# New places for 1111 steps of an attention and mixture-of-experts kernel

## The chip, the cores and the metric

The kernel runs on one core of a Trainium2 chip. The metric is the device time of one launch in microseconds (us). The engines are TensorE (PE, with its weight load PEld), VectorE (DVE), ScalarE (ACT), GpSimd (POOL) and SyncE (SP), which here issues the loads and stores.

## What is computed

For each of 8 batches a memory attention with 8 heads, 576 tokens, head size 64 and 32 memory slots, and then a mixture of 8 experts whose choice sticks from token to token:

```python
a = softmax(phi, axis=tokens)                       # phi: [8, 8, 576, 32]
k_m = einsum('bhsm,bhsd->bhmd', a, k)
v_m = einsum('bhsm,bhsd->bhmd', a, v)
attn = softmax(q @ k_m.T / sqrt(64))                # over the 32 slots
x = (attn @ v_m), heads side by side                # [8, 576, 512]

logits = x @ w_gate                                 # 8 experts
local_gate = sigmoid(x @ w_local)
for s in range(576):
    fresh = argmax(logits[b, s])
    e = fresh if s == 0 or local_gate[b, s] < 0.5 else prev_e
    prev_e = e
    p = softmax(logits[b, s])
    out[b, s] = p[e] * (relu(x[b, s] @ w1[e]) @ w2[e])   # w1: 512x1024, w2: 1024x512
```

## The kernel before

The output of the attention is never formed. The kernel keeps the weights `at` of the attention (128 rows of heads and slots, by 576 tokens) and multiplies w1 of an expert with the keys of memory into G, so that the hidden layer is G times `at`. Both are split into a high and a low half (`Gh`, `Gl`, `ah`, `al`) and each product is made of three. Every batch computes the expert of its first token for all its tokens; a loop behind the program covers batches that need more experts.

The MoE part of a batch is a chain of matmuls on TensorE in rounds. `hidden` makes 12: four with 256 tokens and twelve matmuls each, eight with 320 tokens and six each; ScalarE and VectorE write each result as `h`. `turned` makes 32 (four output parts `dc` by eight chunks, three matmuls of 448 columns each), and behind every eighth VectorE transposes the output into `oT`. `natural` makes 8 more for the first 128 tokens. That is 52 rounds per batch and 68 for the last.

All other work stands as named steps in a table, the string `SCHEDULE`. Its first line is the prologue, run before any round; then one line is run behind each round, most of them empty. A step begins with the number of its batch. The table alone sets the order of the instructions on each engine, since nothing reorders them later; an engine takes its instructions in that order, and each waits for its operands and for the buffer it writes.

The steps that matter here, with the lines in the program: `phi`, `k`, `v` load a batch's inputs (L614), `q 0` and `q 1` sixteen pieces of q (L640), `q0 c` and `q0 d` the last parts of batch 0's q (L675, L669), all on SP's queue. `cm 0` to `cm 2` are a tree of maxima of phi on VectorE (L719), `pm`, `mc`, `pm2`, `cx` carry it across partitions (L736 to L758), `sub` and `dsub` subtract it (L763, on GpSimd and on VectorE), `pkv` sums keys and values on TensorE (L794), `pT` and `kvT` turn them, `pgg` multiplies the gate's weights with them (L866). `qT` transposes q on VectorE (L893), `psc` makes the scores (L925), `turn` transposes them (L938), and `mx`, `sub`, `exp`, `sum`, `inv`, `mul`, `at` are their softmax (L955 to L986). `a`, `z`, `o` and `p` ahead of such a name mean the part of the tokens: `a` the first nine blocks of 32, `z` the last nine; in batch 0 `o` the first block and `p` the next eight. `pl0` and `choice` take the expert of the first token (L1010, L1023 to L1025), `expert` reads it on SP (L1424), `w1` and `w2` load its weights (L1185, L1196), `pg` makes G (L1220) and `G` splits it (L1233, L1235). In batch 0 `pg` comes in four parts: `pg lo`, `pg hi`, `pg 1 lo`, `pg 1 hi`. `split` splits w2 on ScalarE and GpSimd (L1207, L1208). `warm` steps multiply zeros (L694); their results are not used.

Of the kernel before, what the change touches and what calls it, by code (L numbers as in the profile page):

```python
# [82 lines left out]


0 at store, 2 exp 1, 0 g cols, 0 gate 1, 1 a mul, 2 asum, 1 a at


1 ggt, 1 pl0, 2 q 0, 1 a ah, 1 a al, 2 q 1, 1 z psc, 1 choice, 2 pkv 0, 2 pkv 1, 2 sums, 0 gate 0, 1 z turn, 1 expert, 2 rinv, 1 w1 0, 1 w1 1
# [4 lines left out]
1 z mx  # L93
2 z qT 0, 1 z sub
2 z qT 1, 2 kvn, 2 pT, 1 pg 0, 1 w2 0, 0 gate 3, 1 z exp, 2 kvT, 0 gate 2, 1 z sum, 1 z inv, 1 z mul, 1 z at, 1 g pl, 1 g lt, 3 phi, 0 evict, 1 G 0, 2 a qT 0, 2 z psc, 1 pg 1, 1 G 1, 2 z turn, 1 split 0, 1 split 1
2 z mx
1 z ah, 1 z al, 1 split 2
# [8 lines left out]
1 g L  # L110
# [24 lines left out]
3 cx


3 sub 0, 3 exp 0, 3 a qT 0, 2 a ah  # L140
# [3 lines left out]
3 kvn, 1 gate 3

2 split 1, 2 w2 1, 2 split 2  # L150

3 pT, 3 kvT

3 a psc, 3 a turn, 3 z psc, 3 a mx, 2 at store, 3 pgg, 2 split 3, 2 split 4, 3 ggt, 4 phi, 4 colmax
1 g present, 2 split 5, 2 split 6
1 store

3 z turn
3 a sub
2 split 7, 4 q 0, 4 z qT 0
4 q 1
4 pm, 1 row store, 4 mc


3 z mx, 2 g fresh
3 a exp, 3 a sum, 3 a inv, 3 a mul, 3 a at  # L170
# [6 lines left out]
3 z sub, 2 g kept, 3 z exp  # L177
# [4 lines left out]
3 pl0, 2 g carry, 3 choice, 4 pm2  # L182
# [5 lines left out]


4 cx, 3 z sum, 4 sub 0, 3 z inv, 2 g exp, 4 kv, 2 g prob, 2 g cols  # L190

3 a ah, 3 a al

3 z mul, 3 expert, 3 w1 0, 3 w1 1, 3 z at

4 a qT 0

2 kv store, 4 exp 0, 4 sub 1, 4 exp 1, 2 gate 3
2 evict, 2 gate 1, 4 asum, 4 a qT 1, 3 pg 0, 3 G 0, 3 at store, 3 pg 1, 2 gate 2, 3 G 1, 4 pkv 0, 4 pkv 1, 3 w2 0, 4 sums, 3 w2 1, 4 z qT 1, 3 z ah, 2 gate 0
3 split 0, 3 z al, 4 rinv, 5 phi, 3 split 1, 3 split 2  # L200


4 kvn

4 pT, 4 kvT, 3 split 3
3 g pl, 3 split 4, 3 split 5, 3 split 6, 3 split 7, 4 z psc, 2 row store, 4 pgg, 4 ggt, 4 a psc, 4 z turn, 4 z mx, 4 a turn


4 a mx, 4 a sub, 4 a exp
4 a sum
# [11 lines left out]
5 kv, 4 a ah, 4 pl0, 4 choice, 3 g kept, 4 z sub  # L230
# [222 lines left out]

7 evict
# [1202 lines left out]
```

## Time and profile before

| | us |
|---|---|
| median of 3 runs | 391.22 (390.28 to 391.35) |
| profiled execution | 392.12 |
| its span in the profile | 390.3 |
| TensorE busy | 382.3 |
| VectorE busy | 285.2 |
| ScalarE busy | 170.6 |
| GpSimd busy | 157.3 |

The span runs from the first to the last instruction in the trace, and 1.8 us of the profiled execution lie around it. A busy time is the sum over an engine's instructions. An engine with a low share still decides where another engine waits for it; this is read from the waits, the stretch and the timeline, whose rows stand further below.

### The profile page before, as it was taken

The page shows a single profiled execution, that of the slowest core. Times are in us where ns is not written, and L with a number is a line of the kernel's source. Part 1 is how long each engine was busy: PE and PEld are TensorE (multiplying, and loading weights), DVE is VectorE, ACT ScalarE, POOL GpSimd, SP SyncE. Part 2 cuts the span into 40 slices and gives each one's busy share as a digit, 9 for nine tenths or more (in the row PEclk, how much of TensorE's full clock was granted, in tenths as well). Part 3 has the DMA queues.
Part 4 walks back from the last instruction along what each step waited for, and adds up shares of the span by engine and source line. Part 5 has one row for each costly group of instructions (what it writes and reads, how often), then busy time and mean ns, then how long its engine had stood idle before and what let it go on. Part 6 is the DMA issues. An engine that isn't in the chain of part 4 may idle for free. (4 is left out here: it accounts for less than half of the span.)

```text
span 390.3 us, 10303 instructions
## 1 busy us (share of the span) xinstructions
PE 382.3 (98%) x4088; PEld 329.8 (84%) x4088; DVE 285.2 (73%) x700; ACT 170.6 (44%) x430; POOL 157.3 (40%) x166
## 2 busy tenths in 40 slices
PE   8889999999999999999999999999999999999996
PEld 3658989789987998798987998879997998879995
DVE  4488769877968598666787788697896668765651
ACT  2337804276136641466205752357413753148111
POOL 1015940455026461457104673066304861336320
PEclk9989999999999999999999999999999999999999
DMA  7989798899729974997856389488797340584012
GB/s 232 265 285 395 139 265 176 268 351 325 142 101 329 268 171 179 349 304 141 273 215 225 114 165 314 135 322 226 127 359 294 123 109 16 183 267 179 0 36 91
DMA packets 119947, 82.55 MB, mean 211 GB/s; under 512 B 69972, under 2 KB 95320, under 8 KB 119896
## 3 DMA queue, kind: packets, MB, share of 16 engines
q1 hardware_dynamic: 119896, 81.86, 70.0%
q8 instruction: 33, 0.54, 0.6%
q14 instruction: 18, 0.15, 0.1%
HBM read 66.60 MB, written 15.24 MB: 210 GB/s over the span
## 5 line engine op out<-in xcount | busy, mean ns | idle before, releaser
L1208 POOL TENSOR_TENSOR w2l<-raw,w2h 128x512 fp32r<-128x512 f32 x64 | 81.4, 1298 | 49.0 <-ACT w2h L1207 28.4
L1283 PE MATMUL po<-h,w2l 128*128 128x448 f32 (+1 forms) x256 | 93.3, 365 | 0.0
L1285 PE MATMUL po<-h,w2h 128*128 128x448 f32 (+1 forms) x256 | 91.8, 359 | 0.0
L1284 PE MATMUL po<-h,w2h 128*128 128x448 f32 (+1 forms) x256 | 91.8, 359 | 0.0
L1260 DVE SCALAR_TENSOR_TENSOR h<-ph,h 128x320 fp32r<-128x320 f32 (+1 forms) x96 | 52.0, 553 | 32.5 <-ACT h L1259 32.0
L1251 PE MATMUL ph<-ah,Gh 128*128 128x256 f32 (+1 forms) x256 | 73.8, 303 | 0.0
L1251 PE MATMUL ph<-ah,Gl 128*128 128x256 f32 (+1 forms) x256 | 72.2, 296 | 0.0
L1294 POOL TENSOR_TENSOR oT<-oT,gT 128x448 f32<-128x448 f32 (+1 forms) x32 | 29.1, 925 | 85.0 <-ACT gT L1160 40.7
L1259 ACT ACTIVATE h<-ph 128x320 fp32r<-128x320 f32 (+1 forms) x96 | 46.3, 489 | 29.5 <-PE ph L1251 29.3
L1251 PE MATMUL ph<-al,Gh 128*128 128x256 f32 (+1 forms) x256 | 54.9, 295 | 0.0
L1251 PEld LDWEIGHTS ph<-ah,Gh 128*128 128x128 f32 x256 | 48.2, 188 | 4.3 <-issue 1.2
L1283 PEld LDWEIGHTS po<-h,w2l 128*128 128x128 f32 x256 | 48.3, 189 | 4.1 <-issue 0.7
L1285 PEld LDWEIGHTS po<-h,w2h 128*128 128x128 f32 x256 | 48.1, 188 | 3.6
L1284 PEld LDWEIGHTS po<-h,w2h 128*128 128x128 f32 x256 | 48.1, 188 | 3.2
L1251 PEld LDWEIGHTS ph<-ah,Gl 128*128 128x128 f32 x256 | 48.3, 189 | 0.4 <-DVE Gl L1235 0.2
L994 POOL TENSOR_TENSOR al<-at,ah 128x576 fp32r<-128x576 f32 (+1 forms) x18 | 23.7, 1319 | 44.4 <-ACT ah L990 44.2
L1251 PEld LDWEIGHTS ph<-al,Gh 128*128 128x128 f32 x256 | 41.1, 188 | 0.0
L1207 ACT ACTIVATE w2h<-raw 128x512 fp32r<-128x512 f32 x64 | 37.1, 626 | 0.1
L763 POOL TENSOR_TENSOR phi_t<-phi_t,cx 128x384 f32<-128x384 f32 (+1 forms) x13 | 18.5, 1436 | 41.5 <-ACT cx L758 30.0
L965 ACT ACTIVATE sc<-sc 128x576 f32<-128x576 f32 (+2 forms) x18 | 11.3, 631 | 47.6 <-DVE sc L960 47.6
L1268 PE MATMUL po<-w2h,h 128*128 128x512 f32 (+1 forms) x80 | 29.7, 371 | 0.0
L1269 PE MATMUL po<-w2l,h 128*128 128x512 f32 (+1 forms) x80 | 29.5, 369 | 0.0
(157 smaller groups left out, 555.9 us busy)
## 6 DMA issues: line engine op xcount, KB each, us to landing
raw<-in_moe_w_dram SPq DMA_DIRECT2D x34, 512.0 KB, 6.5
raw<-in_moe_w_dram SPq DMA_DIRECT2D x15, 1024.0 KB, 6.9
kv_t<-in_v_dram SPq DMA_DIRECT2D x7, 1152.0 KB, 9.3
kv_t<-in_k_dram SPq DMA_DIRECT2D x7, 1152.0 KB, 6.1
q_t<-in_q_dram SPq DMA_DIRECT2D x112, 72.0 KB, 2.9
out_dram<-oT SPq DMA_DIRECT2D x28, 224.0 KB, 4.0
att_d<-at SPq DMA_DIRECT2D x8, 576.0 KB, 5.7
phi_t<-in_phi_dram SPq DMA_DIRECT2D x7, 576.0 KB, 6.8
```

Source lines behind the costliest of these rows:

```text
L994: (eng or nc.gpsimd).tensor_tensor(out=st.al[:, gs, ss], in0=st.at[:, gs, ss], in1=st.ah[:, gs, ss], op=ALU.subtract)
L1207: nc.scalar.activation(h, src, AF.Copy)
L1208: nc.gpsimd.tensor_tensor(out=l, in0=src, in1=h, op=ALU.subtract)
L1251: nc.tensor.matmul(pv[:, c - c0], lhsT=lt[:, g, cs], rhs=rt[:, g, s0 : s0 + n], start=(i == 0), stop=(i == 5),)
L1259: nc.scalar.activation(hi, pv, AF.Relu)
L1260: nc.vector.scalar_tensor_tensor(out=lo, in0=pv, scalar=0.0, in1=hi, op0=ALU.max, op1=ALU.subtract)
L1268: nc.tensor.matmul(po, lhsT=ht[:, c, 0, ts], rhs=hi, start=(c == 0), stop=False)
L1269: nc.tensor.matmul(po, lhsT=ht[:, c, 0, ts], rhs=lo, start=False, stop=False)
L1283: nc.tensor.matmul(po[:, 0:n], lhsT=lo, rhs=ht[:, c, 0, s1:], start=(c == 0), stop=False)
L1284: nc.tensor.matmul(po[:, 0:n], lhsT=hi, rhs=ht[:, c, 0, s1:], start=False, stop=False)
L1285: nc.tensor.matmul(po[:, 0:n], lhsT=hi, rhs=ht[:, c, 1, s1:], start=False, stop=(c == FC - 1))
L1294: nc.gpsimd.tensor_tensor(out=x, in0=x, in1=g, op=ALU.mult)
```

## The change

The table is replaced: 1111 steps on all engines have new places, none is added to or dropped from the real work. The steps `warm u`, `warm k` and `warm v` (39, 24 and 8 matmuls of 32 columns) are gone; `warm n` (8 of 32 columns) and more `warm b` (one of 512 columns) stand in the prologue instead. `z ah` and `z al` can now be run for one half of the rows, either of `q 0` and `q 1` may come first, and `idle` drains SP three times.

```diff
@@ SCHEDULE @@
...
-1 kvT, 1 z qT 1, 2 sub 1, 2 sub 0, 1 a qT 1, 1 a psc, 1 pgg, 1 a turn
...
+1 pgg, 1 a psc, 2 pm2, 2 cx, 1 a turn, 1 z qT 0, 2 kv, 2 sub 1, 1 a mx
...
     def fetch_q(st, hs):
 
-        if hs.start == 0:
+        if not hasattr(st, "qt"):
             st.qt = pin.tile([P, HG, NB, 32], F32, tag="q", name="q_t", bufs=1)
...
         "warm b": lambda st: warm(1),
-        "idle": lambda st: [nc.sync.drain(), nc.sync.drain()],
-        "warm u": lambda st: warm(39, 32, False),
-        "warm k": lambda st: warm(24, 32, False),
-        "warm v": lambda st: warm(8, 32, False),
+        "idle": lambda st: [nc.sync.drain() for _ in range(3)],
+        "warm n": lambda st: warm(8, 32, False),
...
         STEPS[f"p ah {g}"] = lambda st, g=g: k_ah(st, 0, PB, each[g])
+        STEPS[f"z ah {g}"] = lambda st, g=g: k_ah(st, PB, NB, each[g])
+        STEPS[f"z al {g}"] = lambda st, g=g: k_al(st, PB, NB, gs=each[g])
```

Three places show what moves. The first is SP's order in the prologue, between the gate's weights and the first loads of w1 (`raw1`). Before:

```order
L563 DMA wg_103<-in_moe_w_gate_dram 128x4x8
L675 DMA q0_138<-in_q_dram 128x8x128
L614 DMA phi_t_362<-in_phi_dram 128x4x288
L669 DMA q0e_126<-in_q_dram 32x4x64 x2
L614 DMA phi_t_407<-in_phi_dram 128x4x288
L1424 TENSOR_LOAD ei_358
L1185 ISA
L1185 DMA raw1_461<-in_moe_w1_dram 128x4x256
```

After:

```order
L563 DMA wg_103<-in_moe_w_gate_dram 128x4x8
L614 DMA phi_t_326<-in_phi_dram 128x4x288
L675 DMA q0_138<-in_q_dram 128x8x128
L669 DMA q0e_126<-in_q_dram 32x4x64 x2
L614 DMA kv_t_141<-in_k_dram 128x4x576
L1424 TENSOR_LOAD ei_389
L1185 ISA
L1185 DMA raw1_519<-in_moe_w1_dram 128x4x256
```

Batch 1's phi changes places with the second middle part of batch 0's q, and k of batch 1 (1152 KB) stands where phi of batch 2 stood; that phi now follows behind v of batch 1, and the two halves of w2 behind it. In both orders SP reads the expert ahead of w1.

The second is VectorE in the prologue, from the transpose of the first block's attention weights (`at`) to the softmax of the next eight blocks. Before:

```order
L986 STREAM_TRANSPOSE at_142<-sc_306 128x2x32
L1023 MAX m8_357<-pl0_354 1x8
L1024 MAX_INDEX ei_358<-m8_357,pl0_354 1x8
L1025 TENSOR_SCALAR c0_0_118<-ei_358 1x1
L719 TENSOR_TENSOR tree_367<-phi_t_362 128x512
L719 TENSOR_TENSOR tree_367<-tree_367 128x4x64
L938 STREAM_TRANSPOSE sc_404<-psc_394 128x256
L938 STREAM_TRANSPOSE sc_404<-psc_395 128x256
L955 TENSOR_REDUCE mx_409<-sc_404 128x16
```

After:

```order
L986 STREAM_TRANSPOSE at_142<-sc_313 128x2x32
L719 TENSOR_TENSOR tree_343<-phi_t_326 128x512
L1023 MAX m8_388<-pl0_385 1x8
L1024 MAX_INDEX ei_389<-m8_388,pl0_385 1x8
L1025 TENSOR_SCALAR c0_0_118<-ei_389 1x1
L938 STREAM_TRANSPOSE sc_403<-psc_393 128x256
L938 STREAM_TRANSPOSE sc_403<-psc_394 128x256
L719 TENSOR_TENSOR tree_343<-tree_343 128x4x64
L955 TENSOR_REDUCE mx_450<-sc_403 128x16
```

The first step of batch 1's maximum tree goes ahead of the choice of the expert, the second behind the transposes of the scores. Twelve rows further, a subtraction over two thirds of batch 1's phi (`dsub 0`, L763) now stands between the transposes of the `z` scores and the two instructions that write the first half of `Gl`.

The third is VectorE around the transposes of batch 1's q, in batch 0's `turned` rounds (`oT` is the first of its four output parts). Before:

```order
L1260 SCALAR_TENSOR_TENSOR h_591<-ph_904,h_591 128x320
L740 TENSOR_REDUCE mc_918<-pm_916 128x2
L893 STREAM_TRANSPOSE qT_925<-q_t_839 128x576
L893 STREAM_TRANSPOSE qT_944<-q_t_839 128x576
L1064 TENSOR_REDUCE gmx_946<-L_848 32x18
```

and, twelve rows further, after the rest of the gate's small steps:

```order
L1288 STREAM_TRANSPOSE oT_927<-po_928 128x14x32
L893 STREAM_TRANSPOSE qT_944<-q_t_839 128x576
L893 STREAM_TRANSPOSE qT_925<-q_t_839 128x576
L938 STREAM_TRANSPOSE sc_1027<-psc_1007 128x288
L938 STREAM_TRANSPOSE sc_1027<-psc_1008 128x288
```

After:

```order
L1260 SCALAR_TENSOR_TENSOR h_601<-ph_903,h_601 128x320
L893 STREAM_TRANSPOSE qT_931<-q_t_830 128x576 x2
L1064 TENSOR_REDUCE gmx_954<-L_949 32x18
L1066 TENSOR_TENSOR ex_956<-L_949,gmx_954 32x144
L1068 SCALAR_TENSOR_TENSOR t8_958<-ex_956,code_98 32x144
L1072 TENSOR_REDUCE fr_960<-t8_958 32x18
L938 STREAM_TRANSPOSE sc_989<-psc_975 128x288
L938 STREAM_TRANSPOSE sc_989<-psc_976 128x288
L893 STREAM_TRANSPOSE qT_992<-q_t_830 128x576
L955 TENSOR_REDUCE mx_998<-sc_989 128x18
L1288 STREAM_TRANSPOSE oT_912<-po_913 128x14x32
```

Both transposes of the `a` half of q now stand together ahead of the gate's steps, and the scores of batch 1 are turned before the first `oT` instead of behind it; on TensorE the products of these scores, `a psc`, move from behind round 26 of batch 0 to behind round 18. In the prologue, TensorE has `pm2` far ahead of `pg hi`, six `warm b` between `pg lo` and `pg hi`, and behind `pg hi` only `pg 1 lo` before the hidden layer. Later in the program the steps keep their work and change rounds; in batch 4 the small steps of `g present` (L1145) and in batch 5 `z sub` (L960) come to stand where GpSimd works on the splits of w2.

## Rows read from the trace of the kernel before

**Rows 1.** Page, part 1, whole run: engine, busy us, share, instructions.

```profile
PE 382.3 (98%) x4088; PEld 329.8 (84%) x4088; DVE 285.2 (73%) x700; ACT 170.6 (44%) x430; POOL 157.3 (40%) x166
```

**Rows 2.** Page, part 2: TensorE's busy share in 40 slices, in tenths.

```profile
PE   8889999999999999999999999999999999999996
```

**Rows 3.** Waits of TensorE: engine, line, releaser, us in total, times, longest us.

```profile
PE pm L736 <- DVE cm L719: 1.5, 1, 1.5
```

**Rows 4.** Timeline of the end, TensorE: start, us, engine, line, operation, tiles, count [idle before].

```profile
386.18 0.28 PE L1270 MATMUL po<-w2h,h 128*128 128x256 f32 x1
```

**Rows 5.** Timeline of the prologue, VectorE.

```profile
18.78 0.24 DVE L986 STREAM_TRANSPOSE at<-sc 128x64 f32<-128x64 f32 x1
...
19.46 0.16 DVE L1023 MAX8 m<-pl 1x8 f32<-1x8 f32 x1 [0.43 <-PE pl L1010]
...
19.99 0.14 DVE L1025 TENSOR_SCALAR c<-ei 1x1 f32<-1x1 uint32 x1
...
20.70 0.69 DVE L719 TENSOR_TENSOR tree<-phi_t 128x512 f32<-128x512 f32 x1 [0.56 <-DMA phi_t<-in_phi_dram]
...
21.42 0.43 DVE L719 TENSOR_TENSOR tree<-tree 128x256 f32<-128x256 f32 x1
21.77 0.77 DVE L938 STREAM_TRANSPOSE sc<-psc 128x256 f32<-128x256 f32 x2
...
28.82 0.74 DVE L1235 TENSOR_TENSOR Gl<-pg,Gh 128x256 fp32r<-128x256 f32 x2
```

**Rows 6.** Groups by line and form, VectorE, first 60 us: busy us, mean ns | idle before.

```profile
L763 DVE TENSOR_TENSOR phi_t<-phi_t,cx 128x768 f32<-128x768 f32 x2 | 1.9, 949 | 0.8 <-ACT cx L758 0.8
```

**Rows 7.** Timeline of the prologue, TensorE and its weight load PEld.

```profile
15.81 0.59 PE L694 MATMUL wp<-wz 128*128 128x512 bf16 x2
...
25.01 0.13 PEld L1220 LDWEIGHTS pg<-raw,kvT 64*32 64x32 f32 x2 [0.17 <-DMA raw<-in_moe_w_dram]
...
26.65 1.64 PE L694 MATMUL wp<-wz 128*128 128x32 bf16 x40
...
28.22 1.23 PE L1220 MATMUL pg<-raw,kvT 64*32 64x256 f32 x16
...
29.79 0.79 PE L1220 MATMUL pg<-raw,kvT 64*32 64x256 f32 x16
...
30.50 0.39 PE L1251 MATMUL ph<-ah,Gh 128*128 128x256 f32 x1
```

**Rows 8.** Windows: stretch, length, busy PE, PEld, DVE, ACT, POOL, granted clock, DMA share, GB/s.

```profile
21.00:24.00 3.00, 2.27 (x37) 1.98 (x36) 2.90 (x8) 0.25 (x1) 0.00 (x0) 1.00 0.65 207
24.00:30.00 6.00, 5.27 (x98) 2.70 (x106) 5.83 (x18) 3.89 (x12) 1.59 (x2) 0.73 0.98 330
26.70:30.10 3.40, 3.40 (x68) 1.84 (x73) 3.37 (x9) 2.05 (x8) 1.59 (x2) 0.50 0.95 316
30.10:33.50 3.40, 3.40 (x50) 2.45 (x35) 2.94 (x8) 2.75 (x9) 1.01 (x1) 1.00 1.05 398
```

**Rows 9.** Timeline of batch 0's output products: SP, TensorE, VectorE.

```profile
45.58 4.28 SPq L640 DMA_DIRECT2D q_t<-in_q_dram  x8
...
51.21 0.37 PE L1283 MATMUL po<-h,w2l 128*128 128x448 f32 x1
...
53.34 1.44 DVE L893 STREAM_TRANSPOSE qT<-q_t 128x576 f32<-128x576 f32 x2
...
56.50 0.71 PE L925 MATMUL psc<-qT,kvT 64*32 64x288 f32 x16
```

**Rows 10.** Page, part 6: loads, count, KB each, median us from issue to landing.

```profile
kv_t<-in_k_dram SPq DMA_DIRECT2D x7, 1152.0 KB, 6.1
q_t<-in_q_dram SPq DMA_DIRECT2D x112, 72.0 KB, 2.9
```

**Rows 11.** VectorE at 340 us in the timeline, and that form over the run.

```profile
339.93 1.29 DVE L976 TENSOR_SCALAR sm<-sm 128x18 f32<-128x18 f32 x1
...
L976 DVE TENSOR_SCALAR sm<-sm 128x18 f32<-128x18 f32 x15 | 4.4, 296 | 0.4
```

More of the change, by code (lines that the diff above doesn't have):

```diff
@@ L85 @@
[L85 to L101, printed above, removed]
@@ L148 @@
[L148 to L194, printed above, removed]
@@ L196 @@
[L196 to L218, printed above, removed]
@@ new lines @@
+0 gate 3
+0 store, 1 split 7
+1 g L
+1 g fresh, 2 a psc, 2 a turn, 3 q 1, 3 pm, 3 mc, 1 g kept
+1 g exp, 0 row store
+2 ggt, 2 a mx
+2 a sub, 2 kv store, 2 a exp
+3 pm2, 3 cx, 3 sub 0, 3 exp 0, 3 a qT 0, 3 sub 1, 2 a sum, 2 a inv, 2 a mul
+3 z qT 1
+2 a at
+2 z mx, 1 g carry
+2 pl0, 2 choice
+2 z sub, 2 z exp, 3 exp 1, 1 g prob
+2 expert, 2 w1 0, 1 g cols, 1 gate 1, 3 z qT 0
+3 pkv 0, 2 a ah, 2 w2 0, 2 split 0, 2 split 1, 3 pkv 1, 2 w1 1, 0 kv store, 2 a al, 3 asum, 3 sums, 2 pg 0
+2 z sum, 2 z inv, 2 split 2, 1 g present, 3 rinv
@@ new lines @@
+2 z mul, 3 kvn, 3 pT
+2 z at, 1 gate 2, 2 G 0, 2 g pl, 3 kvT, 1 evict, 3 z psc, 2 g lt, 2 g L, 3 pgg, 4 phi, 4 colmax, 2 z ah, 2 z al, 2 pg 1, 3 ggt, 2 G 1, 3 z turn
+2 w2 1, 2 split 3, 2 split 4, 1 gate 3, 3 a qT 1
+2 split 5, 4 q 0
+3 z mx, 3 a psc, 4 pm, 2 split 6, 1 gate 0, 2 split 7
+3 a turn, 1 store, 3 a mx
+3 z sub
+3 a sub, 3 z exp, 3 a exp
+2 g fresh, 2 at store
+3 z sum
+2 g exp
+4 z qT 0
+3 a sum, 3 a inv
+3 z inv, 3 z mul
+4 mc
+3 a mul
+3 a at
+3 a ah, 4 q 1
+4 kv
+2 g kept
+3 pl0, 4 pm2, 4 cx, 4 sub 0, 4 a qT 0
@@ new lines @@
+3 choice
+2 g carry, 2 g prob
+2 g cols
+3 expert, 3 w1 0
+1 row store
+3 z at
+2 gate 3, 4 sub 1, 4 exp 1, 3 w1 1
+3 w2 0, 4 z qT 1, 4 a qT 1
+3 pg 0, 4 exp 0, 4 asum, 4 pkv 0, 2 gate 1, 3 z ah, 2 evict, 3 a al, 3 split 0, 3 G 0, 3 pg 1, 4 pkv 1, 4 sums, 3 G 1, 2 gate 0, 4 rinv, 4 kvn
+5 q 0, 5 phi, 3 z al, 3 split 1, 4 pT, 4 kvT, 3 split 2, 5 colmax
+3 at store
+3 w2 1, 2 gate 2, 4 pgg, 4 ggt, 4 a psc, 3 g pl, 3 split 3, 3 split 4, 5 kv, 3 split 5, 2 row store, 5 pm, 5 q 1, 5 a qT 0, 5 mc, 4 a turn, 3 g lt
@@ new lines @@
+5 a turn, 4 split 2, 4 split 3
+5 a mx, 3 store, 4 split 4, 4 split 5
+4 g lt
+5 a sub
+4 split 6
+5 a exp
+5 pgg, 4 split 7, 5 a sum, 3 evict, 5 a inv, 5 a mul, 6 pm
+6 q 0, 6 mc, 5 ggt, 5 a at, 5 z sum
+4 g L
+5 z inv, 5 pl0, 5 choice, 6 pm2, 6 cx, 6 sub 1, 5 expert, 5 w1 0
+6 z qT 0
+3 g present, 6 sub 0
+6 exp 0
+4 kv store
+6 exp 1
+4 g fresh, 4 g kept, 4 g carry
+6 pkv 0, 5 pg 0, 5 w1 1, 4 g exp
+6 q 1
+5 G 0
+4 g prob, 4 g cols
+5 a ah
+5 z mul, 4 gate 1
+4 gate 2
+5 z at, 5 z ah
+6 asum, 5 w2 0, 5 a al, 5 z al, 4 gate 3, 3 row store, 5 split 0, 5 split 1, 5 at store, 5 idle
@@ new lines @@
+6 pkv 1, 6 sums, 4 gate 0, 6 a qT 0, 5 split 2, 4 evict, 6 z qT 1, 5 pg 1, 6 rinv, 6 kvn, 6 a qT 1, 5 G 1, 5 g pl, 6 pT, 6 kvT
+5 split 3, 5 w2 1, 5 split 4, 7 q 0, 5 split 5, 6 a psc, 7 q 1, 5 split 6, 5 kv store, 6 a turn, 4 g present, 6 a mx, 5 split 7, 6 a sub, 6 z psc
+6 z turn
+6 a exp
+6 a sum
+7 phi, 7 a qT 0
+7 colmax, 7 a qT 1, 5 g lt
+4 store, 6 z mx
+6 a inv
+7 kv, 6 pgg, 6 ggt, 7 pm
+6 a mul, 7 mc
+5 g L
+6 a at, 6 pl0, 6 z sub, 6 z exp, 6 choice, 6 expert, 6 w1 0, 7 pm2, 7 cx, 7 sub 1
@@ L447 @@
+7 split 7
+6 row store
+0 pairs
+7 g L, 7 g fresh, 7 g kept, 7 g carry
+7 at store
+7 g exp
+7 g prob
 7 g cols
 6 kv store
[L452 removed]
 7 evict
[L461 to L475 removed]
+7 gate 2, 7 gate 3, 7 gate 0, 7 gate 1, 7 store, 7 row store, 7 g present, 7 list, 7 last 0, 7 last 1
 """
```

207 lines of the change are left out of this document (85 added, 122 removed).

## The prediction

> **What bounds the kernel now.** The first thing to read is the line of busy times: TensorE (PE) is busy 382.3 us of a span of 390.3, VectorE (DVE) 285.2, and ScalarE and GpSimd well under half of it [rows 1]. The second is the strip of 40 slices: PE shows a 9 in every slice from the fourth to the last but one, and is below that only at both ends [rows 2]. The third is the list of PE's waits: it has four lines of one wait each, the longest of 1.5 us [rows 3], and all four belong to steps of the prologue. The last is the end: the last matmul begins at 386.18 us and takes 0.28 [rows 4]; behind it only one eviction and its store are left. So the program is a prologue of 30.50 us, up to the first matmul of the hidden layer [rows 7], and then 356 us (386.5 - 30.5) in which TensorE never waits. The change adds and drops no matrix product, so from the first hidden matmul on it can gain nothing on TensorE. What is left is
>
> time after = time before + shift of the first hidden matmul + new waits of TensorE behind it.
>
> The profiled execution took 392.12 us, 1.8 more than its span and 0.9 above the median of the runs shown. I take the sum as a difference and set it on the median, 391.22.
>
> **The prologue, VectorE.** Before, the first hidden matmul needs Gl, the low half of the product of w1 and the keys, which VectorE writes from 28.82 [rows 5]. VectorE is packed from the transpose `p turn` at 21.77 to there, 7.05 us. Ahead of that turn stand the choice of the expert (ending at 20.13) and two tree steps of batch 1's column maximum, of which the first waited 0.56 for its phi until 20.70 [rows 5]. After, the loads of phi and of the second middle part of q change places, so phi should come before the tree step wants it. The tree step (0.69) moves ahead of the choice, the second one behind the turn, and a subtraction `dsub 0` of 0.95 [rows 6] comes in from later. The output transpose ended at 19.02 before; with the tree step right behind it, then the choice at its old pace (19.46 to 20.13, 0.67), the turn starts at 19.15 + 0.70 + 0.67, about 20.5. The stretch to Gl grows by the second tree step (0.35, from 21.42 to 21.77) and by `dsub 0`: 20.5 + 7.05 + 0.35 + 0.95 = 28.85. So VectorE's date for Gl is where it was; 1.3 us won ahead are spent on work that came from later.
>
> **The prologue, TensorE.** Before, TensorE was later than Gl. Forty small warming matmuls (1.64 us), the second quarter of the product (1.23 instead of 0.79) and the transpose `pm2` ran in a stretch where the granted clock was 0.50 [rows 8], then came `pg 1 lo` (0.79), and the first hidden matmul at 30.50 [rows 7]. After, `pm2` stands far ahead, the small warming matmuls there are replaced by wide ones, six of them between the first and the second quarter, and behind the second quarter stands only `pg 1 lo`. Two wide ones took 0.59 in the prologue, the first of them with its start [rows 7]; I take 0.25 each at the full clock. The first quarter, at the first piece of w1 (25.6, below), ends at 26.4; six times 0.25 and two products of 0.79 make 29.5 if they follow each other in full, less where the overlap of a product with its neighbours (0.71 from 29.79 to 30.50) is counted. The first hidden matmul may then begin when Gl of the first half is nearly there: 28.85 + 0.37 for one of the two instructions (0.74 for both), so about 29.2, and TensorE's own date is about the same. That is a **gain of 1.3 us**. The second round's Gl follows four VectorE instructions later, by 31.6, about when TensorE, after a round of 1.4 and a block of 0.8, asks for it; I put 0 there.
>
> **The prologue, loads.** The gain needs w1 in time. The SP queue now carries k of batch 1 (1152 KB [rows 10]) ahead of w1, where the phi of batch 2 stood, half as large. At the 316 to 398 GB/s of the stretches that are full [rows 8], the extra 590 thousand bytes take 1.5 to 1.9 us. Between 21 and 24 us the DMA engines are busy 0.65, so 1.05 us are free there [rows 8], and the queue ahead of w1 is issued before that gap. So w1 would land 0.4 to 0.9 later than now. Its first piece landed at 25.0 [rows 7]; its third is wanted by `pg 1 lo` at about 28.4, and its bytes behind the first (2 x 512 KB) take 2.6 to 3.3 us: 25.0 + 0.6 + 2.9 = 28.5. It just holds; I take 0 here and keep the upper end, 1.4, for a rival.
>
> **Behind the prologue.** Most of the 1111 places move on engines that have slack, and then cost nothing: the 700 instructions of VectorE fill 73% [rows 1], and TensorE waited for none of them in 356 us. One place has no such cover. The scores of batch 1, `1 a psc`, move from behind round 26 of batch 0 to behind round 18. Round 18 ended at 51.21 before, the scores began at 56.50 [rows 9]. After, `pT` and `pgg` of batch 1 stand ahead of them too, two and sixteen small products; I put 0.5 us, less than the 0.71 of the sixteen larger ones of the scores [rows 9]. So they stand at 51.21 + 0.5 - 1.3, about 50.4. They need all sixteen loads of q of batch 1, two transposes of VectorE (1.44 together, 0.72 each [rows 9]), and the second half of the loads only after half of the sixteen matmuls (0.35): the last load must land by 50.4 + 0.35 - 0.72 = 50.0. Before, the last eight were issued from 45.58 to 49.86, 0.54 each [rows 9], so the last at about 49.3; the middle load lands 2.9 us after its issue [rows 10]: 52.2, and by 53.34, when the last transpose began, at the latest. The bytes ahead of them are the same in both programs, so the queue can be ahead by no more than the 1.05 us of the gap that it fills: 52.2 - 1.05 = 51.15. TensorE would **wait 1.1 us** at the scores, 2.3 if the load lands as late as the bound 53.34 - 1.05, nothing if issue to landing is 1.7 us. What is queued behind the waiting transposes on VectorE is batch 0's gate and batch 1's turn; the output turn of step 8 comes two rounds later, and TensorE has a second output bank until then, so this wait passes on to nobody else.
>
> **GpSimd and VectorE.** The trace shows VectorE instructions that last far longer than their like while GpSimd runs a subtraction: at 339.93 one of 128x18 took 1.29 us, where the fifteen of its form take 0.30 on average, this one among them [rows 11]. After, batch 4's small gate steps and batch 5's subtraction of the maximum come to stand among GpSimd's w2 splits, right ahead of VectorE's writes of the hidden layer. One such hold is 1.0 us, and none made TensorE wait before. I take 0 and keep 1.1 as an upper end.
>
> Sum: 391.22 - 1.3 + 1.1 = **391.0 us**.
>
> **The rivals.**
> (1) *The gain stays whole.* The q loads land by 50.0. For it: the 2.9 us are a median over all 112 such loads [rows 10], and a queue that holds nothing else could be quicker. Against it: SP issues them one after the other, and no new order speeds that up. 391.22 - 1.3 = 389.9; with Gl another 0.4 earlier 389.5.
> (2) *w1 waits behind k.* If the gap is not filled and all 1.9 us of k's extra time fall on w1, its third piece lands at 25.0 + 1.9 + 2.9 = 29.8, 1.4 after it is wanted, and the gain is gone. The scores then stand at 51.8 and want q by 51.4; without the 1.05 of the gap it lands at 52.2: 391.22 - 1.3 + 1.4 + 0.8 = 392.1. The Trainium skill, "DMA: Bandwidth & Descriptors", section "Queues, rings and completion order", speaks for this one: on each DMA engine descriptors are consumed in ring order, and a load counts as done only when every engine that carries it has reported. By that rule w1 cannot pass k, however late it is wanted. This trace shows only that the gap is there before it, and whether it is enough is what the estimate above rests on.
> (3) *Slower: the scores wait for q in full.* The mechanism is the one place above. It decides from the point at which the wait exceeds the gain, that is when the last q load lands after 50.0 + 1.3 = 51.3. If it lands as before's bound less the gap, 52.3, with the gain intact: 391.22 - 1.3 + 2.3 = 392.2. If it lands at 53.3, because w1 and all behind it come no sooner than now: 391.22 - 1.3 + 3.3 = 393.2.
> (4) *The dent of the clock.* The stretch 26.7 to 30.1 ran at 0.50, the next one, full of hidden matmuls, at 1.00 [rows 8], that is at 1.2 and 2.4 GHz. TensorE worked through the whole of it, on warming and on the product of w1; why the grant fell there no row says. The new warming matmuls stand elsewhere, so the dent can go (no further gain, since Gl sets the date), stay, or come later. If it stays, the six wide matmuls take 3.0, the second quarter 1.23, and the hidden layer begins at 26.4 + 3.0 + 1.23 + 0.71 = 31.3; the scores then find q there: 391.22 + 0.8 = 392.0. If it falls on a stretch that is all hidden matmuls, 3.4 us at half speed cost 1.7: 391.0 + 1.7 = 392.7.
> (5) *A hold on VectorE reaches TensorE* once: 391.0 + 1.1 = 392.1.
>
> **How the numbers follow.** A measurement of this kernel can tell about 0.3% (1.17 us) from no change, so faster is below 390.05 and slower above 392.39. Chances: forecast (0.4 to 1.5 us of wait) 0.35; (1) 0.24; (2) 0.10; (3) 0.15, half of it beyond 392.4; (4) 0.11, of it 0.04 for the later dent; (5) 0.05. Below 390.05 lies rival 1, and a first hidden matmul still earlier than 29.2: 0.26. Above 392.39 lie half of (3), the later dent of (4), a part of (5) when it adds to a longer wait, and what I have not seen in 1111 moved steps: 0.20. The rest is 0.54. The forecast's own range is 390.3 to 391.4; the one that holds the time 8 times in 10 goes from rival 1 with the earlier Gl, 389.4, to the first case of rival 3 with a hold of half a microsecond, 392.7, which is also the later dent of rival 4.
>
> **What would show it.** In the changed kernel's trace: the first hidden matmul at 29.2 (29.0 to 30.0), its release by Gl on VectorE, `p turn` at 20.5, the first w1 piece at 25.0 to 26.0; in the list of TensorE's waits, one for `psc` of batch 1 near 50.4 with VectorE's `qT` as releaser, 1.1 us; no wait of more than 0.3 us after 60 us. A first hidden matmul at or after 30.3 makes the gain wrong; no wait at `psc` makes the give-back wrong; several waits of half a microsecond behind 60 us make the claim of slack wrong, and then the whole sum.

## The result

The changed kernel is **slower**: 396.14 us median (395.37 to 398.32, 6 runs) against 391.06 (390.28 to 391.67, 6 runs) for the kernel before, a ratio of 1.014 with a 95% interval of 1.0112 to 1.0168. I had forecast 391.0 with a range of 389.4 to 392.7.

The page of the changed kernel, its line of busy times and two strips of 40 slices (in tenths):

```profile
PE 386.8 (98%) x4090; PEld 328.1 (83%) x4090; DVE 291.2 (74%) x700; ACT 171.9 (44%) x431; POOL 159.8 (41%) x166
...
PE   8999999999999999999999999999999999999996
...
PEclk9999999999999999999999999999999999999999
```

TensorE shows 4.5 us more of busy time than in [rows 1], for the same matrix products. Its waits are listed with total, count and longest, in us:

```profile
PE wp L692 <- DVE zeros L533: 1.3, 1, 1.3
PE ph L1251 <- DVE h L1260: 0.4, 1, 0.4
PE pm L752 <- DVE mc L740: 0.4, 1, 0.4
PE pkv L794 <- ACT ex L1075: 0.3, 1, 0.3
```

Two of the four lie in the prologue, as all four did before [rows 3]. Most of the lost time is thus in no line of this list. The first and the last of the hidden and output products, in the timeline of the changed kernel (start, length, line, operation, tiles, count):

```profile
28.19 1.59 PE L1220 MATMUL pg<-raw,kvT 64*32 64x256 f32 x32
...
29.06 0.74 DVE L1235 TENSOR_TENSOR Gl<-pg,Gh 128x256 fp32r<-128x256 f32 x2
29.08 0.21 PEld L1220 LDWEIGHTS pg<-raw,kvT 64*32 64x32 f32 x16 [0.58 <-DVE phi_t L763]
...
29.70 0.38 PE L1251 MATMUL ph<-ah,Gh 128*128 128x256 f32 x1
```

```profile
389.43 0.28 PE L1270 MATMUL po<-w2h,h 128*128 128x256 f32 x1
```

The first hidden matmul is 0.8 us earlier than in [rows 7], the last product 3.25 later than in [rows 4]. From the first to the last it is 359.7 us instead of 355.7, so the loss lies in the stretch that TensorE fills.

To see where, I divided TensorE's stream into the matmuls of the MoE rounds and the blocks of side work between them (scores, sums, parts of G, transposes). The block's time is what lies between its neighbours beyond their own pace. A run of 64x32 tiles is an unbroken row of matmuls that use 64x32 of TensorE's 128x128 array; a block can hold several. Second executions of both kernels gave a second trace each:

| | first hidden matmul | first to last product | side blocks | their time | runs of 64x32 tiles |
|---|---|---|---|---|---|
| before, two traces | 30.50, 29.25 | 355.7, 355.5 | 34 | 52.4, 52.4 | 21 |
| after, two traces | 29.70, 30.22 | 359.7, 360.2 | 38 | 55.8, 56.3 | 28 |

So 3.4 to 3.9 of the 4.0 to 4.7 us lie in blocks of the same work. Two things make them longer: they are cut more often, and in some TensorE waits.

**A cut has a price.** Scores `psc` and gate product `pgg` of batch 1 in the kernel before, in one block:

```profile
56.20 0.37 PE L1285 MATMUL po<-h,w2h 128*128 128x448 f32 x1
56.50 0.71 PE L925 MATMUL psc<-qT,kvT 64*32 64x288 f32 x16
57.01 0.25 PE L866 MATMUL pgg<-wg,kvT 64*32 64x9 f32 x16
57.18 0.47 PE L1283 MATMUL po<-h,w2l 128*128 128x448 f32 x1
```

The same scores of batch 2 in the changed kernel, with a 128x128 transpose behind them, and a `pgg` that stands alone:

```profile
96.16 0.36 PE L1285 MATMUL po<-h,w2h 128*128 128x448 f32 x1
96.45 0.71 PE L925 MATMUL psc<-qT,kvT 64*32 64x288 f32 x16
97.10 0.33 PE L736 MATMUL pm<-ident,cm 128*128 128x128 f32 x1
```

```profile
316.90 0.27 PE L866 MATMUL pgg<-wg,kvT 64*32 64x9 f32 x16
317.10 0.41 PE L1251 MATMUL ph<-ah,Gh 128*128 128x320 f32 x1
```

The next instruction follows the scores after 0.51 us when it has the same tile, 64x32, and after 0.65 when it is a 128x128 one. Around a block, the product ahead of it and the one behind it take about 0.1 us more each than their pace (0.29 or 0.30 to the next start instead of 0.20). A `pgg` of sixteen products behind scores adds 0.04 us to their block (first experiment below), alone it costs 0.40. A single 128x128 transpose alone between rounds makes a block of 0.11 us (`pm` at 47.46 us in the kernel before), so the interruption as such is the smaller part. The Trainium skill has a rule that fits: "TensorEngine Tiling (Array Packing)", section "Tiling Modes", says that a change of the tiling mode, not just of the tile, drains TensorE. It gives no price; the rows do, and they agree with it, though none shows the drain itself.

**And TensorE waits.** In the changed kernel's trace, the last q of batch 1 releases its transpose at 50.11, and the scores behind it take 0.91 us to the next instruction instead of 0.65:

```profile
50.11 0.78 DVE L893 STREAM_TRANSPOSE qT<-q_t 128x576 f32<-128x576 f32 x1 [1.67 <-DMA q_t<-in_q_dram]
...
50.65 0.98 PE L925 MATMUL psc<-qT,kvT 64*32 64x288 f32 x16
```

The sums of batch 2 wait at 60.5 for v; the releaser that the row names is a ScalarE instruction that does not write their operands, and v, issued at 49.42, lands 11.3 us later, at 60.7:

```profile
60.94 0.82 PE L794 MATMUL pkv<-kv_t,phi_t 64*32 64x128 f32 x41 [0.35 <-ACT ex L1075]
```

A VectorE product beside a GpSimd subtraction takes 1.74 us instead of 0.76; the transpose behind it, and `g pl` on TensorE, come late:

```profile
121.47 1.43 POOL L994 TENSOR_TENSOR al<-at,ah 128x576 fp32r<-128x576 f32 x1
...
121.78 1.74 DVE L982 TENSOR_TENSOR sc<-sc,sm 128x576 f32<-128x576 f32 x1
...
124.39 0.41 PEld L1035 LDWEIGHTS pl<-at,ggt 128*32 128x32 f32 x14 [0.16 <-DVE at L986]
```

And ScalarE, busy with splits and `g L`, is late for the hidden layer of batch 6:

```profile
312.17 0.97 ACT L1052 ACTIVATE L<-lt 32x45 f32<-32x45 f32 x4
...
313.04 1.54 ACT L1259 ACTIVATE h<-ph 128x512 fp32r<-128x512 f32 x3
...
314.39 0.38 PE L1251 MATMUL ph<-ah,Gh 128*128 128x256 f32 x1 [0.45 <-DVE h L1260]
```

Those four are 0.26, 0.41, 0.29 and 0.60 us.

### The profile page after: what moved, and what is told of

It reads as the page before. It is cut to its first block, busy times and chain, and to the rows that moved or that the text cites. A ratio compares the mean times of both kernels' runs of the same rounds, so it can differ in the third digit from the quotient of the medians.

```text
span 393.6 us, 10343 instructions
## 1 busy us (share of the span) xinstructions
PE 386.8 (98%) x4090; PEld 328.1 (83%) x4090; DVE 291.2 (74%) x700; ACT 171.9 (44%) x431; POOL 159.8 (41%) x166
## 5 line engine op out<-in xcount | busy, mean ns | idle before, releaser
L1208 POOL TENSOR_TENSOR w2l<-raw,w2h 128x512 fp32r<-128x512 f32 x64 | 82.9, 1319 | 55.2 <-ACT w2h L1207 43.2
L1294 POOL TENSOR_TENSOR oT<-oT,gT 128x448 f32<-128x448 f32 (+1 forms) x32 | 30.0, 949 | 73.2 <-ACT gT L1160 55.6
L763 POOL TENSOR_TENSOR phi_t<-phi_t,cx 128x384 f32<-128x384 f32 (+1 forms) x13 | 18.5, 1444 | 69.3 <-ACT cx L758 35.6
L1288 DVE STREAM_TRANSPOSE oT<-po 128x448 f32<-128x448 f32 (+1 forms) x32 | 20.0, 624 | 26.2 <-PE po L1285 22.4
L1268 PE MATMUL po<-w2h,h 128*128 128x512 f32 (+1 forms) x80 | 30.2, 378 | 0.0
L1270 PE MATMUL po<-w2h,h 128*128 128x512 f32 (+1 forms) x80 | 29.6, 370 | 0.0
```

The source lines that it names most:

```text
L1208: nc.gpsimd.tensor_tensor(out=l, in0=src, in1=h, op=ALU.subtract)
L1268: nc.tensor.matmul(po, lhsT=ht[:, c, 0, ts], rhs=hi, start=(c == 0), stop=False)
L1270: nc.tensor.matmul(po, lhsT=ht[:, c, 1, ts], rhs=hi, start=False, stop=(c == FC - 1))
L1294: nc.gpsimd.tensor_tensor(out=x, in0=x, in1=g, op=ALU.mult)
```

## The experiments

All were timed against the kernel before on the same chip. The theory, A: the loss is the price of cuts plus waits of TensorE that the new places bring; the prologue gives nothing back. Rivals: the loss is waits alone; or it sits in the prologue and its loads.

**Cuts, first try.** In the table of before, `pgg` of batches 1 to 6 two rounds behind its scores; for batch 1:

```diff
-1 kvT, 1 z qT 1, 2 sub 1, 2 sub 0, 1 a qT 1, 1 a psc, 1 pgg, 1 a turn
+1 kvT, 1 z qT 1, 2 sub 1, 2 sub 0, 1 a qT 1, 1 a psc, 1 a turn
...
+1 pgg
```

> The kernel before with one thing altered: in batches 1 to 6 the sixteen small products `pgg` stand two rounds behind the scores instead of right behind them. Theory A (each separate run of 64x32-tile matmuls on TensorE between the full 128x128 ones has a fixed price: in the traces the sixteen products of `psc` take 0.51 us when `pgg` follows and 0.65 when a 128x128 product follows, a block of `psc` and `pgg` costs 0.89, of `psc` alone 0.85, of `pgg` alone 0.40): six more runs at about 0.36 us, +2.2 us against before, about 393.2. Rival B (only the work counts, and the changed kernel loses its time to waits for loads and for VectorE and ScalarE): within 0.3 us of before.

Measured: 403.6 us, ratio 1.0303 (1.0283 to 1.0323). The price came out in the rows (batch 1: blocks of 846 and 403 ns instead of one of 886), but in batches 3 and 6 `pgg` fell among hidden rounds, where its PSUM banks were not free:

```profile
140.56 0.27 PE L866 MATMUL pgg<-wg,kvT 64*32 64x9 f32 x14 [1.85 <-DVE h L1260]
```

and behind each such wait the granted clock fell. Stretches of this run (length, busy time and count of PE, PEld, DVE, ACT and POOL, granted clock, DMA share, GB/s):

```profile
138.50:141.90 3.40, 0.47 (x17) 0.29 (x16) 3.37 (x5) 1.01 (x3) 3.06 (x3) 0.92 0.83 135
142.00:148.10 6.10, 6.06 (x18) 5.58 (x19) 3.33 (x5) 1.09 (x4) 1.28 (x1) 0.50 0.94 311
148.30:151.00 2.70, 2.70 (x16) 2.46 (x14) 0.29 (x1) 0.29 (x2) 0.00 (x0) 1.00 0.60 237
```

TensorE worked 0.47 of 3.4 us and then ran at 0.50, 1.2 GHz, for six. The total says nothing on the price of cuts; the rows show a long wait with half the clock behind it, which costs more than its length.

**Joining cuts in the changed kernel.** `pgg` of batches 5, 6 and 7 moved behind their scores, two blocks of batch 5 joined:

```diff
-5 z turn, 4 split 1, 5 z mx, 4 w2 1, 5 z sub, 5 z exp, 4 g pl, 5 a psc, 4 pg 1, 4 G 1, 4 at store
+4 g pl, 5 z psc, 5 z turn, 4 split 1, 5 z mx, 4 w2 1, 5 z sub, 5 z exp, 5 a psc, 5 pgg, 4 pg 1, 5 ggt, 4 G 1, 4 at store
...
-7 kv, 6 pgg, 6 ggt, 7 pm
+7 kv, 7 pm
```

> The changed kernel with four of its runs of small-tile matmuls joined to a neighbour: `pgg` of batches 5, 6 and 7 right behind scores of their batch, and `z psc` of batch 5 into the same block as `a psc`. Theory A: four runs fewer at 0.36 us, 1.4 us faster than the changed kernel, about 394.7. Rival B: no difference from the changed kernel, 396.1.

403.08 us, 1.0311 (1.0287 to 1.0335). Both expectations failed: the joined `pgg` waited 2.9 us for its banks in batch 7, in batch 5 it and the part of G behind it came about 3 us late, and two stretches of 3.4 us at half the clock followed. A cut could not be undone alone where the banks were taken.

**The new prologue on the old table.** The first line and rounds 1 to 4 are the changed kernel's; the end of them:

```diff
...
+
+0 w2 1
+
+1 q 0, 0 g L, 0 split 4
 0 split 5, 0 split 6
```

> The prologue and the first four rounds of the changed kernel, and the table of before for the rest. Theory: the new prologue is a gain by itself, the first hidden matmul at 29.7 as in the changed kernel instead of 30.5, and the sums of keys and values joined with the gate's product in one block save another 0.2: 1.0 us faster than before, about 390.1. Rival (k ahead of w1 delays w2 and q behind it, and a wait gives the gain back): 391.0 with a new wait of TensorE between 36 and 60 us.

393.43 us, 1.0056 (1.0041 to 1.0072): slower than before, where I expected a gain. The first hidden matmul stood at 30.29, and TensorE waited 0.26 us for `h` at 46.8 and 0.70 at 227.3 in the middle of a group of matmuls, with "issue" as releaser, for a reason that no row shows. So the new prologue with its loads made the old table about 2.2 us slower by the ratio, and the two waits are only a part of that; the changed kernel's traces have no wait at these two places.

**Four waits taken away at once**, each by moving a step; for instance

```diff
-2 sub 0, 2 exp 0, 1 a at, 1 z psc, 1 z turn, 1 z mx, 1 a ah, 2 pkv 0, 2 q 0, 1 pl0, 1 choice, 1 expert, 1 w1 0
+2 sub 0, 2 exp 0, 1 a at, 1 z psc, 1 z turn, 1 z mx, 1 a ah, 2 q 0, 1 pl0, 1 choice, 1 expert, 1 w1 0
...
-2 pkv 1, 2 sums, 2 rinv, 2 kvn, 0 g prob, 1 a al, 0 g cols, 0 gate 0, 1 z inv
+2 pkv 0, 2 pkv 1, 2 sums, 2 rinv, 2 kvn, 0 g prob, 1 a al, 0 g cols, 0 gate 0, 1 z inv
```

> The changed kernel with its four waits of TensorE taken away: the scores of batch 1 two rounds later (wait for q, 0.26 us in the trace), the first part of batch 2's `pkv` at the place of the second (wait for v, 0.41), `g pl` of batch 2 behind `pg 1` (wait for VectorE held by GpSimd, 0.29), and `g L` of batch 6 six rounds later (ScalarE late with the hidden layer, 0.60). Theory A: these four are all the waiting there is, 1.6 us faster than the changed kernel by its trace, about 394.6. Rival B (waits are the whole loss, and larger in most executions than in the one profiled, which was the shortest): 4 to 5 us faster, 391 to 392.

398.19 us, 1.0192 (1.0178 to 1.0206): no gain. The wait for ScalarE in batch 6 was gone, but `pl0` of batch 1, now without the sums ahead of it, waited 0.4 us for `at`, and behind the place to which I had moved `g pl` of batch 2 the hidden layer waited 1.1 us for VectorE. Both expectations failed.

**Halves.** The changed table up to round 156 with the old one behind it, and the other way round (diffs left out: whole parts of the table are taken over).

> The changed kernel's table up to the end of batch 2's rounds (round 156), and before's table from there. Theory A, worked out from the two traces (0.36 us for each more run of small-tile matmuls, plus the waits of TensorE): two more runs, 0.7, and the waits for q, v and `at`, 1.0; the new prologue gains at most what the profiled execution of before lost to its dent of the clock, which another execution need not have: 0 to -0.8. So 0.9 to 1.7 us over before, about 392.3. Rival B (the loss sits in the prologue and the loads of batches 0 to 2): the whole 5 us, 396.

> The other half: before's table up to round 156 and the changed kernel's from there. Theory A: five more runs of small-tile matmuls, 1.8 us, and the wait for ScalarE at batch 6's hidden layer, 0.6: 2.4 us over before, about 393.3, with few differences between executions. Rival B: no more than 0.5 us over before.

The first half gave 395.3 us, 1.0102 (1.0083 to 1.0121), more than A's 0.9 to 1.7 and less than B's 5. The second gave 402.74, 1.0295 (1.027 to 1.032), and doesn't count: where the two tables meet, TensorE waited 3.0 us for a maximum of batch 5, for which the kernel before never waits and the changed one 0.2 us in one of two executions, and 3.4 us at half the clock followed.

**Both kernels once more.**

> The kernel before once more, for a second trace. If the dent of the granted clock at 26.7 to 30.1 us belongs to the program, it is there again and the first hidden matmul is at 30.5. If it belongs to that one execution, the clock stays at 1.00, the first hidden matmul is at 29.2 to 29.7, and the span is about 389.1, which is what the median of its times less 1.8 gives.

> The changed kernel once more, for a second trace. Its six times lay between 395.4 and 398.3, and the profiled one was the shortest. Theory: the executions differ in TensorE's waits for loads (q, k and v of batches 1 to 3) and for VectorE and ScalarE; a longer one shows the same sequence of matmuls with the same price of each block, and larger or more waits. Rival: the blocks themselves take longer.

390.67 and 396.39 us. The kernel before, in its second trace:

```profile
29.25 0.39 PE L1251 MATMUL ph<-ah,Gh 128*128 128x256 f32 x1
```

```profile
24.00:25.40 1.40, 1.31 (x33) 0.70 (x34) 1.32 (x5) 0.65 (x3) 0.00 (x0) 1.00 1.08 360
25.50:28.80 3.30, 2.94 (x64) 1.77 (x71) 3.30 (x8) 1.97 (x6) 1.59 (x2) 0.50 1.09 396
28.90:32.00 3.10, 3.10 (x48) 2.21 (x33) 2.63 (x7) 2.44 (x8) 1.01 (x1) 1.00 1.03 401
```

The dent of the clock is there again, as the first case expected, yet the hidden layer begins at 29.25, as the second did: the dent came 1.2 us sooner than in [rows 8], and so did the work in it, since the first piece of w1 landed at 24.05 instead of 24.97. So 30.50 was this execution's date, not the program's. Nor does the dent belong to the program: of all eight traces with the old prologue, those of the experiments counted, three have it (this one, [rows 8] and the old prologue on the new table below), and of eight with the new one none. Of the five without it the first hidden matmul stands at 29.08 to 29.89. The changed kernel's second trace has other waits than its first, two of them where the first had none:

```profile
178.60 0.30 PE L736 MATMUL pm<-ident,cm 128*128 128x128 f32 x1 [0.21 <-DVE cm L699]
...
181.44 0.30 PE L749 MATMUL pm<-ident,mcw 128*128 128x128 f32 x1 [0.31 <-DVE sc L938]
```

**More cuts in the old table**, away from scarce banks: `pgg` of batches 1, 2 and 5, and the sums of batches 1, 2, 4, 5 and 7 in two parts.

```diff
-2 colmax, 1 pkv 0, 1 pkv 1, 1 sums, 1 rinv, 1 q 0, 0 g L, 0 split 4
-0 split 5, 0 split 6
+2 colmax, 1 pkv 0, 1 q 0, 0 g L, 0 split 4
+1 pkv 1, 1 sums, 1 rinv, 0 split 5, 0 split 6
```

> The kernel before with more, shorter blocks of side work on TensorE and nothing else: `pgg` of batches 1, 2 and 5 two rounds behind its scores, where no PSUM bank is short, and the sums `pkv` of batches 1, 2, 4, 5 and 7 cut in two, one round apart. Theory A, from the blocks of the traces: a `pgg` that stands apart costs 0.363 us more each (846 + 403 ns against 886 in the earlier run with `pgg` apart), a cut `pkv` about 0.2: 3 x 0.36 + 5 x 0.2 = 2.1 us over before, about 393.1, with no new wait of TensorE. Rival B (blocks as such cost nothing): within 0.3 of before.

395.69 us, 1.0118 (1.0097 to 1.014): 4.7 us instead of 2.1. In its trace a cut of the sums costs 0.41, not 0.2 (batch 1: blocks of 1503 and 1319 ns instead of 2413), which makes 3 x 0.36 + 5 x 0.41 = 3.1 in all; the blocks of side work grew by 4.2, the rest being mostly waits, 0.7 of them for `at` at 78.4.

**Two repairs**: scores of batch 5 joined, `g L` of batch 6 later.

```diff
-4 z at, 3 gate 0, 3 gate 1, 4 z ah, 5 z psc
-...
-5 z turn, 4 split 1, 5 z mx, 4 w2 1, 5 z sub, 5 z exp, 4 g pl, 5 a psc, 4 pg 1, 4 G 1, 4 at store
+4 z at, 3 gate 0, 3 gate 1, 4 z ah
+...
+4 g pl, 5 z psc, 5 a psc, 5 z turn, 4 split 1, 5 z mx, 4 w2 1, 5 z sub, 5 z exp, 4 pg 1, 4 G 1, 4 at store
```

> The changed kernel with two repairs: the scores `z psc` and `a psc` of batch 5, two blocks in rounds 203 and 205, stand in one, and `g L` of batch 6 comes six rounds later, so that ScalarE is free for the hidden layer. Theory A: 0.36 and 0.60 us less in the trace, 1.0 us faster than the changed kernel, about 395.3. Rival B (these waits only move on): within 0.3 of the changed kernel, 396.2.

396.7 us, 1.0158 (1.0134 to 1.0182), as rival B had it: the wait of 0.60 was gone, the joined scores were shorter, but waits of 0.6 and 0.4 us for VectorE's `qT` and `h` came in.

**Fewer blocks in the old table**, to beat both kernels; for batch 1:

```diff
-2 z qT 1, 2 kvn, 2 pT, 1 pg 0, 1 w2 0, 0 gate 3, 1 z exp, 2 kvT, 0 gate 2, 1 z sum, 1 z inv, 1 z mul, 1 z at, 1 g pl, 1 g lt, 3 phi, 0 evict, 1 G 0, 2 a qT 0, 2 z psc, 1 pg 1, 1 G 1, 2 z turn, 1 split 0, 1 split 1
+2 z qT 1, 2 kvn, 2 pT, 1 pg 0, 1 w2 0, 0 gate 3, 1 z exp, 2 kvT, 0 gate 2, 1 z sum, 1 z inv, 1 z mul, 1 z at, 3 phi, 0 evict, 1 G 0, 2 a qT 0, 2 z psc, 1 pg 1, 1 g pl, 1 G 1, 1 g lt, 2 z turn, 1 split 0, 1 split 1
```

> The kernel before with its blocks of side work joined further at two places: the gate's product `g pl` of batch 0 right behind the sums of batch 1 instead of in a block of its own, and that of batch 1 behind both parts of G instead of between them. Theory A: 0.2 and 0.3 us less on TensorE, 0.5 us faster than before, about 390.6. Rival B: same as before, or slower if the gate's steps that follow come late.

392.82 us, 1.0047 (1.0031 to 1.0064), slower. `g pl` of batch 0 joined to the sums did save 0.17 us (a block of 3106 ns for 862 and 2413), but without `g pl` between them the scores of batch 2 and the second part of G came too soon, and TensorE waited 1.4 us in and right behind that block (of batch 1).

**The old prologue on the new table.**

> The changed kernel with the prologue and the first four rounds of before. In the ten traces so far the first hidden matmul stands at 29.25 to 30.50 us with the old prologue (mean 29.8 of four) and at 29.50 to 30.31 with the new one (mean 30.0 of six). Theory A: the two prologues are worth the same, the separate `g pl` costs 0.2: 396.2 to 396.6, as the changed kernel. Rival B (the new prologue is a gain of about 1.3 us that the rest hides): 397.5. Rival C (the new order of loads, k ahead of w1, is what delays q and v of batches 1 and 2): 1 us faster than the changed kernel, 395.2.

398.75 us, 1.0198 (1.0172 to 1.0224), above all three expectations. The first hidden matmul stood at 30.70, the latest of the old prologue so far; the sums of batches 1 and 7 waited 1.1 and 0.6 us more. Since the place where the tables meet adds a wait of its own (for GpSimd's `asum` of batch 1), the run doesn't decide between the prologues.

**Five clean cuts in the old table**: `pgg` of batches 2 and 5, the sums of 1, 4 and 7.

> The kernel before with five cuts of side work at places where the earlier runs showed no new wait: `pgg` of batches 2 and 5 two rounds behind its scores, and `pkv` of batches 1, 4 and 7 in two parts, one round apart. The prices are now those read from the trace of the run with more cuts: 0.36 us for a `pgg` apart, 0.41 for a cut `pkv`. Theory A (a cut costs its price and no more): 2 x 0.36 + 3 x 0.41 = 1.95 us over before, about 393.0, in its trace and in its median. Rival B (moving steps of a tuned table costs about 2 us whatever is moved, by waits in the executions that no trace of ours shows): 395 or more, with a trace that shows the 1.95 alone.

393.26 us, 1.0047 (1.0032 to 1.0062): 2.2 us in the medians for an expected 1.95, and 2.1 more in the blocks of its trace. A holds, and B with its 4 us or more does not. Batch 1's sums in two blocks, and batch 2's scores and `pgg` apart, in its timeline:

```profile
40.47 1.38 PE L794 MATMUL pkv<-kv_t,phi_t 64*32 64x128 f32 x80
...
42.86 1.16 PE L794 MATMUL pkv<-kv_t,phi_t 64*32 64x128 f32 x64
```

```profile
96.01 0.72 PE L925 MATMUL psc<-qT,kvT 64*32 64x288 f32 x16
96.66 0.33 PE L736 MATMUL pm<-ident,cm 128*128 128x128 f32 x1
...
98.15 0.27 PE L866 MATMUL pgg<-wg,kvT 64*32 64x9 f32 x16
98.35 0.47 PE L1283 MATMUL po<-h,w2l 128*128 128x448 f32 x1
```

0.65 us for the scores and 0.20 for `pgg`, as in the changed kernel, from the old table.

**Two waits of the changed kernel, with no step of TensorE moved**: `g L` of batch 6 later, and three splits of batch 2 out of the way of VectorE's product.

```diff
-3 pkv 0, 2 a ah, 2 w2 0, 2 split 0, 2 split 1, 3 pkv 1, 2 w1 1, 0 kv store, 2 a al, 3 asum, 3 sums, 2 pg 0
-...
-2 z sum, 2 z inv, 2 split 2, 1 g present, 3 rinv
+3 pkv 0, 2 a ah, 2 w2 0, 3 pkv 1, 2 w1 1, 0 kv store, 2 a al, 3 asum, 3 sums, 2 pg 0
+...
+2 z sum, 2 z inv, 1 g present, 3 rinv
```

> The changed kernel with two of TensorE's waits taken away by other means than before, and no cut undone: `g L` of batch 6 six rounds later (in both traces of the changed kernel TensorE waits 0.60 us for the hidden layer behind it), and the first three splits of batch 2's w2 five and three rounds later, so that GpSimd does not run beside VectorE's product `z mul` (1.74 us there, 0.76 elsewhere), behind which TensorE waits 0.14 to 0.29 for `at`. Theory A (waits are the part of the loss that is not price of cuts): 0.7 to 0.9 us faster than the changed kernel, about 395.5, and both waits gone from the trace. Rival B (as with the earlier repairs, the wait comes back at another place): within 0.3 of the changed kernel, 396.3.

399.95 us, 1.0208 (1.0166 to 1.025), its runs between 396.3 and 402.1. Both waits were gone from its trace, and VectorE's product, now with no GpSimd work beside it, took 0.74 us. But the first hidden matmul came at 31.60 (the first piece of w1 landed at 27.90 instead of 25.30 in the changed kernel's first trace), and other waits had come, as this one for `at` of batch 2, where the changed kernel's two traces had none:

```profile
112.22 0.24 PE L1010 MATMUL pl<-ggt,at 128*1 128x8 f32 x4 [1.02 <-DVE at L986]
```

Put together, the traces of one table show what its executions differ in. For each block that six traces share, take the shortest as its price. With the old table (the two executions and four variants of it: five cuts, more cuts, fewer blocks and the new prologue, at blocks not altered), the two executions of the kernel before lie 0.06 and 0.07 us above the sum of the shortest. With the new table (its two executions and four variants: the two runs that took waits away, the two repairs and the old prologue), they lie 1.2 and 1.7 us above it, at nine blocks that are late in some executions and not in others: the scores of batch 1 (0 to 1.2 us), the sums of batch 2 (0 to 0.6), `pl0` and `g pl` of batch 2 (0 to 1.1 and 0 to 1.3), two blocks of batch 5's maximum (0 to 0.7 and 0 to 0.5), and three more.

The sum of the loss is then, as an estimate: the price of cuts, 54.6 - 52.3 = 2.3 us by the shortest blocks (seven runs of 64x32 tiles more, at 0.33); waits in blocks, 1.2 and 1.7; the hidden rounds 0.7, of it 0.6 the wait for ScalarE; the first hidden matmul 0.5 later on average (eight traces with the new prologue, 29.50 to 31.60, mean 30.17; eight with the old, 29.08 to 30.70, mean 29.70, the variants counted; the two sets overlap, so that this half microsecond is uncertain). That is 4.7 to 5.2 us, for a difference of 5.1 between the medians. That cuts cost this much each is shown by the experiment with five of them; the 2.3 itself is read from the rows, since no run undid the cuts alone. The waits are shown by rows of two executions, while each attempt to take them away brought others, so that it stays open what this table would cost without them. Nor is the share of the prologue settled: on the old table it cost 2.2 us by itself, more than the 0.5 here.

## Why the prediction was wrong

**The formula had no term for cuts.** "Time after = time before + shift of the first hidden matmul + new waits" follows from "the change adds and drops no matrix product, so from the first hidden matmul on it can gain nothing". The same products can take more time: in more and shorter blocks they cost 2.3 us. This was the largest single term, and the sum had it at nothing. The trace of before had the price: its parts of G and its scores have two lengths each, by what follows. One part of G in that trace takes 0.88 us to the next start, ahead of 64x32 work, and the next 1.09, ahead of a 128x128 product:

```profile
120.60 1.09 PE L1220 MATMUL pg<-raw,kvT 64*32 64x512 f32 x16
121.48 2.21 PE L794 MATMUL pkv<-kv_t,phi_t 64*32 64x128 f32 x143
...
123.62 1.16 PE L1220 MATMUL pg<-raw,kvT 64*32 64x512 f32 x16
124.71 0.39 PE L1251 MATMUL ph<-ah,Gh 128*128 128x256 f32 x1
```

**The gain of 1.3 us was measured against one execution.** The first hidden matmul at 30.50 [rows 7] was 1.25 us later than in the second trace, and the profiled execution was 0.9 us above the median, as I had noted. I then set the difference on the median all the same. In the changed kernel it stood at 29.70 and 30.22, half a microsecond and a whole one past my 29.2. VectorE was nearly on its date: `p turn` at 20.58 for 20.5, Gl ready for the second hidden matmul by 29.43. What came late was the third piece of w1, which I had at 28.5 ("It just holds; I take 0 here"): issued behind k at 22.27, it landed at 28.97, and the weight load of `pg 1 lo`, idle for 0.58 us, began at 29.08 (its row stands in the section on the result; the releaser named there is a VectorE instruction that does not write its operands). In the second trace it landed at 29.49, and there the list of waits names it:

```profile
PE pg L1220 <- DMA raw<-in_moe_w_dram: 0.8, 1, 0.8
```

So the step that failed is the one that rival 2 doubted, w1 behind k, with a landing at 29.8. In the eight traces with the old prologue this piece lands at 27.20 to 29.15 (mean 28.3), in the eight with the new one at 28.43 to 30.86 (mean 29.3). That k ahead of w1 is the cause is argued from the order of the loads; no run moved k alone. Against a typical 29.7, the gain is nothing.

**The wait at the scores of batch 1** came at the predicted place, released by `qT` and ultimately by q, with 0.26 and 0.11 us instead of 1.1. The last q released VectorE at 50.11 instead of the estimated 51.15, but not because it landed faster, as the first rival had it: it took 3.3 us from its issue, more than the 2.9 of [rows 10].

```profile
46.77 1.56 SPq L640 DMA_DIRECT2D q_t<-in_q_dram  x1
```

SP began this issue at 46.77, 2.6 us before the date that follows from [rows 9] (49.36), where the sum allowed a lead of 1.05; in the second trace of the kernel before it already began at 48.58. So the bound on the queue's lead failed. The size is no constant either: with two repairs the same scores lost 1.2 us, with the old prologue on the new table nothing.

**"Most of the 1111 places [...] cost nothing"** was read from the old order, in which TensorE waited for no one behind the prologue. That shows the slack of the old order and none of the new. The waits for v, for `at` and for ScalarE stand in no rival; with the hidden rounds they made 1.9 to 2.4 us of the sum above, where the prediction had 1.1 at one place. GpSimd's hold on VectorE was a rival, at another place and with 1.1 us; it cost 0.29 and 0.14, in batch 2.

**The clock** went the way of the harmless branch: no dent in either trace of the changed kernel, and no gain from it. TensorE's late date before was laid to the dent, yet the second trace of before has the dent and the early date.

## What to carry to other kernels

Where one engine is full, count not only its work but how often that work changes kind: the sequence of tile shapes is part of the cost, and a step may be free where it stands and cost 0.4 us two rounds later. Set a gain read from one execution against the spread of that date over several, before adding it to a median. And a table in which the bound engine waits for nobody is evidence about that table alone: for each moved step on it, ask what it must find ready at its new place.
